# Loads, statistics, transposes and filler matmuls rearranged at the start of an attention and MLP kernel

**Chip, cores, metric.** One NeuronCore of a Trainium2 chip. The metric is the device time of one execution in us; medians are over the runs named. The profile is that of one execution.

## The reference, cut to what matters

One block with adaptive layer norms: grouped-query attention (32 q heads, 8 cached K/V heads, head size 128, 2048 tokens, width 512) and a gated MLP with a spatial matmul.

```python
mod = (silu(c) @ w_mod).reshape(c.shape[0], 6, 1, -1)      # w_mod: 512 x 3072
sa, ca, ga, sb, cb, gb = (mod[:, i] for i in range(6))
h = layernorm(x) * (1 + ca) + sa
x = x + ga * attention(h, k_cache, v_cache, wq, wo)        # q = h @ wq, scores, softmax, @ v, @ wo
h = layernorm(x) * (1 + cb) + sb
x = x + gb * gmlp(h)
```

Before the first score, all of this has to happen: x tile 0 is loaded and normalised, the columns of `sa` and `ca` (a 512 x 1024 part of `w_mod`) are computed, the tile is transposed and modulated, and multiplied with `wq`.

## The kernel before

128 units (8 K/V heads x 16 token tiles) with 8 slots each. In a slot, TensorE (PE) computes 2 QK matmuls of 128x512, ScalarE (ACT) takes the exponential of the 1024 scores, and PE does the PV matmuls of the unit before. What stands in `at(unit, slot, f)` is put ahead of QK in that slot, what stands in `fill[unit, slot]` behind PV. Below, "exp 4" is the exponential of slot 4 of unit 0, if no other unit is named, and a bank is one of the buffers in PSUM into which PE writes. In the traces the work of an engine stands in the order of the program, so what waits holds up what is behind it: the cast of q, whose input is ready at 10.69 us, starts at 11.48, behind the statistics of tile 1.

```python
nc.scalar.dma_start(out=c_bf[:], in_=c_dram)
nc.scalar.dma_start(out=x_sb[:, 0, :], in_=x_dram[:, 0, :])
for i in range(2):                                   # 512 rows of 1 KB each
    part = slice(i * D, (i + 1) * D)
    nc.sync.dma_start(out=wmod_a[:, :, part], in_=wmod_dram[:, :, part])
# ... sync queue then: half of K, wq, x tiles 1 to 3, other half of K, v, the rest of x, wo

warm(14)                                             # matmuls on zeros, results unused
xns0 = ln1_norm(0, 1, ln1_stats(0, 1))
mod_columns(0, wmod_a, 0)                            # 32 matmuls 128x1
ln1_turn(0, 1, xns0, on_act=(1, 3))                  # 4 transposes, modulated on DVE and ACT
# ... 8 transposes of K, copied out by ACT
warm(2)
first["r1"] = ln1_stats(1, 1)                        # tile 1: bn_stats, bn_aggr on DVE, rstd on GpSimd
for fn in qproj(0, list(range(REP)), 0, P, two_engines=True):
    fn()                                             # 16 matmuls; cast half on DVE, half on ACT
first["x1"] = ln1_norm(1, 1, first["r1"])
first["r2"] = ln1_stats(2, 2)
# ...
def first_turn():
    ln1_turn(1, 1, first["x1"])                      # transposes of tile 1
    first["x2"] = ln1_norm(2, 2, first["r2"])
at(0, 1, first_turn)
at(0, 4, lambda: ln1_turn(2, 2, first["x2"]))        # transposes of tiles 2 and 3
fill[0, 0] = [lambda: warm(1)]
fill[0, 2] = [lambda: warm(1)]
fill[0, 3] = qproj(0, list(range(REP)), P, P)        # q of tile 1
fill[0, 6], fill[0, 7], fill[1, 0] = rest_q[0:4], rest_q[4:10], rest_q[10:16]
# ...
ln1_at(1, (1, 1), (1, 5), (1, 7))                    # tiles 4 to 7: statistics, norm, transposes
```

## Time and profile before

| | before |
|---|---|
| median | 1328.3 us (6 runs, 1328.22 to 1329.56) |
| span of the profiled run | 1326.9 us |
| PE busy | 1303.0 us (98%) |
| first QK matmul | 12.33 us |
| first QK of unit 1 | 21.23 us |

From unit 1 on PE has almost no gap, so only the first 30 us matter. A row of the order of time has the start, the duration, the engine (PEld is PE's weight load), the line, the operation, output<-input, the shapes and the count; in brackets the engine's idle time ahead of it and what ended it. The chain and the rows that carry the argument stand in the prediction. One more row, from the order of time of PE in the kernel before, marks the first QK of unit 1:

```profile
21.23 0.59 PE L928 MATMUL s_ps<-qT,kT 128*128 128x512 bf16 x2
```

### The profile page before, as it was taken

The page shows a single profiled execution, that of the slowest core. Times are in us where ns is not written, and L with a number is a line of the kernel's source. Part 1 is how long each engine was busy: PE and PEld are TensorE (multiplying, and loading weights), DVE is VectorE, ACT ScalarE, POOL GpSimd, SP SyncE. Part 2 cuts the span into 40 slices and gives each one's busy share as a digit, 9 for nine tenths or more (in the row PEclk, how much of TensorE's full clock was granted, in tenths as well). Part 3 has the DMA queues.
Part 4 walks back from the last instruction along what each step waited for, and adds up shares of the span by engine and source line. Part 5 has one row for each costly group of instructions (what it writes and reads, how often), then busy time and mean ns, then how long its engine had stood idle before and what let it go on. Part 6 is the DMA issues. An engine that isn't in the chain of part 4 may idle for free.

```text
span 1326.9 us, 27682 instructions
## 1 busy us (share of the span) xinstructions
PE 1303.0 (98%) x12140; PEld 859.3 (65%) x12346; DVE 472.7 (36%) x1166; ACT 1077.4 (81%) x1061; POOL 48.8 (4%) x92
## 2 busy tenths in 40 slices
PE   8999999999999999999999999999999999999997
PEld 5666666666666666666666666666666666644444
DVE  5532222222222222222222222222222566793444
ACT  5898999999999999999999999999999999650000
POOL 1100000000000000000000000000000000120000
PEclk9999999999999999999999999999999999999999
DMA  5461021102111121111110211121101111154200
GB/s 159 102 146 29 17 49 37 33 17 53 21 30 36 34 37 37 29 37 37 33 33 17 53 37 29 21 52 21 33 14 21 25 34 33 29 115 83 64 21 27
DMA packets 146512, 57.59 MB, mean 43 GB/s; under 512 B 136176, under 2 KB 142448, under 8 KB 146384
## 3 DMA queue, kind: packets, MB, share of 16 engines
q1 hardware_dynamic: 139584, 37.19, 14.8%
q0 software_dynamic: 4208, 16.39, 4.5%
q8 instruction: 98, 1.61, 0.5%
q10 hardware_dynamic: 2592, 2.16, 0.5%
q14 instruction: 30, 0.25, 0.1%
HBM read 21.37 MB, written 2.10 MB: 18 GB/s over the span
## 4 chain that ended last, share of the span: by engine, by line
PE 97%; issue 1%; DVE 1%; DMA 1%; ACT 0%; SPq 0%; POOL 0%
PE s_ps L928 35%; PE o_ps L950 35%; PE misc L1290 7%; PE misc L889 7%; PE misc L982 6%; PE s_ps L1136 2%; PE s_ps L1175 2%; PE o_ps L1311 1%; DMA x_sb<-in_A_x_dram 1%; PE s_ps L1311 0%; DVE bnst L691 0%; ACT pT L935 0%; PE misc L1052 0%; DVE qT L901 0%; DVE xn L680 0%
## 5 line engine op out<-in xcount | busy, mean ns | idle before, releaser
L935 ACT ACTIVATE pT<-s_ps 128x1024 bf16<-128x1024 f32 x1024 | 1043.6, 1024 | 86.0 <-PE s_ps L928 11.3
L950 PEld LDWEIGHTS <-pT 128*128 128x128 bf16 x8192 | 548.5, 98 | 241.2
L950 PE MATMUL o_ps<-v,pT 128*128 128x129 bf16 x8192 | 631.5, 220 | 0.0
L928 PE MATMUL s_ps<-qT,kT 128*128 128x512 bf16 x2048 | 608.9, 379 | 12.4 <-ACT qT L903 1.6
L961 DVE RECIPROCAL rall<-o_ps 128x2 f32<-128x2 f32 x256 | 43.6, 170 | 743.9 <-PE o_ps L950 743.8
L928 PEld LDWEIGHTS <-kT 128*128 128x128 bf16 x2048 | 199.3, 98 | 121.8 <-issue 3.6
L889 PE MATMUL misc<-hT,wq_g 128*128 128x512 bf16 (+2 forms) x482 | 167.4, 365 | 0.2
L982 PE MATMUL misc<-wo_g,oT 128*128 128x512 bf16 x385 | 145.9, 379 | 0.0
L962 DVE TENSOR_TENSOR onorm<-o_ps,rall 128x256 bf16<-128x256 f32 x256 | 108.6, 424 | 9.0 <-DVE rall L961 0.3
L1290 PE MATMUL misc<-wsp,z 128*128 128x512 bf16 (+2 forms) x555 | 100.5, 336 | 0.6 <-issue 0.3
L901 DVE CAST qT<-misc 128x512 bf16<-128x512 f32 (+1 forms) x128 | 86.7, 677 | 7.4 <-PE misc L889 7.3
L1290 PEld LDWEIGHTS <-z 128*128 128x128 bf16 x560 | 50.6, 98 | 48.5
L995 DVE TENSOR_TENSOR xacc<-misc,xacc 128x512 f32<-128x512 f32 x112 | 76.0, 679 | 0.0
L889 PEld LDWEIGHTS <-wq_g 128*128 128x128 bf16 x544 | 51.5, 98 | 1.5 <-DMA wq_g<-in_A_wq_dram 0.6
L982 PEld LDWEIGHTS <-oT 128*128 128x128 bf16 x512 | 50.1, 98 | 0.7
L1305 DVE TENSOR_TENSOR gb<-misc,bsp_bc 128x512 bf16<-128x512 f32 (+1 forms) x28 | 18.4, 658 | 59.2 <-PE misc L1290 59.2
L1136 PE MATMUL s_ps<-win_sb,hT 128*128 128x448 bf16 x128 | 27.0, 352 | 0.1
L1146 ACT ACTIVATE z<-s_ps 128x896 bf16<-128x896 f32 x16 | 14.7, 917 | 14.9 <-PE s_ps L1136 14.9
L1175 PE MATMUL s_ps<-hT,win_sb 128*128 128x512 bf16 x109 | 24.3, 379 | 0.2
L691 DVE BATCH_NORM_STATS2 bnst<-x_sb 128x6 f32<-128x512 bf16 x32 | 21.8, 682 | 3.1 <-DMA x_sb<-in_A_x_dram 2.6
L1183 ACT ACTIVATE z1T<-s_ps 128x1024 bf16<-128x1024 f32 x14 | 14.3, 1024 | 10.1 <-PE s_ps L1175 9.1
L708 POOL DMA_DIRECT2D wq_g<-in_A_wq_dram x7 | 5.3, 750 | 420.9 <-PE misc L889 420.9
(79 smaller groups left out, 280.1 us busy)
## 6 DMA issues: line engine op xcount, KB each, us to landing
wq_g<-in_A_wq_dram POOLq DMA_DIRECT2D x7, 512.0 KB, 4.0
v<-in_A_v_cache_dram POOLq DMA_DIRECT2D x7, 512.0 KB, 6.5
wo_g<-in_A_wo_dram POOLq DMA_DIRECT2D x7, 512.0 KB, 4.8
oT<-onorm SPq DMA_TRANSPOSE x128, 2.4
wsp<-in_w_mod_dram POOLq DMA_DIRECT2D x1, 2048.0 KB, 9.3
out_dram<-yout ACTq DMA_DIRECT2D x15, 128.0 KB, 1.7
win_sb<-in_B_w_in_dram POOLq DMA_DIRECT2D x1, 1792.0 KB, 7.7
x_sb<-in_A_x_dram SPq DMA_DIRECT2D x3, 512.0 KB, 6.1
```

Of the source, the lines that this page charges most:

```text
L889: nc.tensor.matmul(ps[0][:, o0 : o0 + n], lhsT=wqs[g][:, dt, hh * DH : (hh + 1) * DH], rhs=hTs[ch][:, dt, c0 : c0 + n], start=(dt == 0), s ...
L901: nc.vector.tensor_copy(out=dst[:, 0:cut], in_=src[:, 0:cut])
L928: nc.tensor.matmul(s_ps[:, h * 512 : (h + 1) * 512].rearrange("p (r q) -> p r q", r=REP), lhsT=groups[g]["kT"][:, kt * P : (kt + 1) * P], ...
L935: nc.scalar.activation(out=pTs[u][:, 2 * i : 2 * i + 2, :], in_=s_ps[:].rearrange("p (k q) -> p k q", k=2), func=ACT.Exp, scale=inv_sqrt_dh,)
L950: nc.tensor.matmul(o_ps[:, hh % 2, 0 : DH + 1], lhsT=pTs[u][:, kt, hh * P : (hh + 1) * P], rhs=groups[g]["v1"][:, kt, 0 : DH + 1], start=( ...
L961: nc.vector.reciprocal(out=rall[:, c0 : c0 + 2], in_=o_ps[:, :, DH])
L962: nc.vector.tensor_tensor(out=onorms[u][:, hh - 1 : hh + 1, :], in0=o_ps[:, :, 0:DH], in1=rall[:, c0 : c0 + 2].unsqueeze(2).to_broadcast([ ...
L982: nc.tensor.matmul(X_ps[:], lhsT=oTs[u][:, hh, :], rhs=groups[g]["wo"][:, hh, :], start=(hh == 0), stop=(hh == REP - 1),)
L995: nc.vector.tensor_tensor(out=xaccs[j][:], in0=X_ps[:], in1=xaccs[j][:], op=ALU.add)
L1136: nc.tensor.matmul(ps[0][:, hf * 512 : hf * 512 + FC], lhsT=h2Ts[j // CT][:, dt, (j % CT) * P : (j % CT + 1) * P], rhs=win_sb[:, dt, FH + ...
L1175: nc.tensor.matmul(ps[0][:, k * 512 : (k + 1) * 512], lhsT=win_sb[:, dt, f * P : (f + 1) * P], rhs=h2Ts[2 * ch2 + k][:, dt, :], start=(dt ...
L1290: nc.tensor.matmul(g_ps[:, :n], lhsT=z2[:, st, f * P : (f + 1) * P], rhs=wsp[t][:, st, c0 : c0 + n], start=(st == 0), stop=(st == NT - 1 a ...
```

## The change

Intent: get x tile 0 and the modulation weight sooner, keep PE's clock up with fillers, and let work that waits stand behind work that is ready.

```diff
-    nc.scalar.dma_start(out=x_sb[:, 0, :], in_=x_dram[:, 0, :])
-    for i in range(2):
-        part = slice(i * D, (i + 1) * D)
-        nc.sync.dma_start(out=wmod_a[:, :, part], in_=wmod_dram[:, :, part])
+    nc.sync.dma_start(out=x_sb[:, 0, :], in_=x_dram[:, 0, :])
+    nc.sync.dma_start(out=wmod_a[:], in_=wmod_dram[:, :, 0 : 2 * D])
...
-    warm(2)
-    first = {}
-    first["r1"] = ln1_stats(1, 1)
+    warm(1)
...
     for fn in qproj(0, list(range(REP)), 0, P, two_engines=True):
         fn()
+    warm(2)
+    first = dict(r1=ln1_stats(1, 1))
+    ln_stats(mv1, 2, x_sb[:, 2, :])
     first["x1"] = ln1_norm(1, 1, first["r1"])
-    first["r2"] = ln1_stats(2, 2)
+    ln_stats(mv1, 3, x_sb[:, 3, :])
+    first["r2"] = rstd_of(mv1[:, 2:4, :], 2, "ln1")
...
-    at(0, 1, first_turn)
-    at(0, 4, lambda: ln1_turn(2, 2, first["x2"]))
-    fill[0, 0] = [lambda: warm(1)]
-    fill[0, 2] = [lambda: warm(1)]
+    at(0, 2, first_turn)
+    at(0, 5, lambda: ln1_turn(2, 2, first["x2"]))
+    for i in (0, 1, 2, 4):
+        fill[0, i] = [lambda: warm(1)]
...
-    fill[0, 6], fill[0, 7], fill[1, 0] = rest_q[0:4], rest_q[4:10], rest_q[10:16]
+    fill[0, 6], fill[0, 7], fill[1, 0] = rest_q[0:5], rest_q[5:11], rest_q[11:16]
```

## The prediction

> **What bounds the kernel now.** I read the page of the whole run first, then the busy time per stretch, and last the order of instructions and the chain that ended last, both in the first 30 us.
>
> ```profile
> span 1326.9 us, 27682 instructions
> PE 1303.0 (98%) x12140; PEld 859.3 (65%) x12346; DVE 472.7 (36%) x1166; ACT 1077.4 (81%) x1061; POOL 48.8 (4%) x92
> ```
>
> TensorE (PE) is busy for 1303.0 of 1326.9 us. The loop is not touched by the change, so at stake are the 23.9 us in which PE is idle. The busy time per stretch says where they lie (first columns: length, then PE):
>
> ```profile
> 0.00:10.00 10.00, 8.44 (x66) 4.11 (x68) 3.40 (x14) 2.74 (x5) 1.69 (x10) 1.00 0.87 249
> 10.00:20.00 10.00, 6.96 (x61) 4.01 (x59) 6.83 (x19) 6.48 (x9) 1.75 (x4) 1.00 1.05 275
> 20.00:30.00 10.00, 9.17 (x94) 6.50 (x92) 6.30 (x16) 8.50 (x10) 1.28 (x2) 1.00 0.01 3
> ```
>
> PE's idle time before 30 us is 1.56 + 3.04 + 0.83 = 5.4 us. In the first stretch most of its busy time is filler, so the useful ceiling is somewhat larger than the idle time there, but all that the change can win is a few us of 1328: 2% would be 26.6 us. The order of time shows what PE waits for (start, duration, engine, line; in brackets the idle time ahead and what ended it):
>
> ```profile
> 9.62 1.07 PE L889 MATMUL misc<-hT,wq_g 128*128 128x128 bf16 x16
> 10.65 0.69 DVE L691 BATCH_NORM_STATS2 bnst<-x_sb 128x6 f32<-128x512 bf16 x1 [1.66 <-DMA x_sb<-in_A_x_dram]
> 11.38 0.18 DVE L692 BATCH_NORM_AGGREGATE mv<-bnst 128x2 f32<-128x6 f32 x1
> 11.48 0.39 DVE L901 CAST qT<-misc 128x256 bf16<-128x256 f32 x1
> 11.90 0.37 ACT L903 CAST qT<-misc 128x256 bf16<-128x256 f32 x1 [1.45 <-DVE qT L901]
> 12.33 0.59 PE L928 MATMUL s_ps<-qT,kT 128*128 128x512 bf16 x2 [1.64 <-ACT qT L903]
> ...
> 17.31 0.38 PE L835 MATMUL misc<-ident,xn 128*128 128x128 bf16 x4 [0.42 <-DVE qT L901]
> ...
> 17.53 1.03 PE L928 MATMUL s_ps<-qT,kT 128*128 128x512 bf16 x4
> 18.16 4.73 ACT L935 ACTIVATE pT<-s_ps 128x1024 bf16<-128x1024 f32 x5 [1.39 <-PE s_ps L928]
> ```
>
> Two stalls. **First:** the q projection ends at 9.62 + 1.07 = 10.69, but VectorE (DVE) casts q only at 11.48, because the statistics of x tile 1 stand ahead of it in DVE's order, and that tile lands only at 10.63. The ScalarE (ACT) half follows the DVE half one after the other, and the first QK matmul starts at 12.33. **Second:** in slot 4 of the first unit the transposes of x tiles 2 and 3 stand ahead of the QK matmul; they wait for the q cast to free a PSUM bank, so ACT has no scores for 1.39 us. That the tile's load lies on the path that ends last, the chain confirms (start, duration):
>
> ```profile
> 3.27 7.36 DMA x_sb<-in_A_x_dram
> 10.65 0.70 DVE bnst L691
> 11.56 0.32 DVE qT L901
> 11.90 0.38 ACT qT L903
> 12.33 0.61 PE s_ps L928 x2
> ```
>
> **What the Trainium skill says.** (1) "TensorE: Matmul & The Clock Gate", Engine queue depths: ScalarE and VectorE are strict FIFO. The trace agrees: DVE's cast, ready at 10.69, waits behind statistics until 11.48. (2) The same page, Part 1: cold matmuls of N=512 start 426.7 ns apart, and the clock rises after one busy window of about 3.4 us, that is free-running. The trace agrees: warm-up matmuls start 0.43 us apart, and full clock is granted from 6.85 us on; it holds through PE's 1.64 us idle. So the fillers are insurance, and here there is no clock loss for them to win back. (3) "DMA: Bandwidth & Descriptors", Issuing engines are not separate DMA queues: another issuing engine saves only sequencer time. So moving x tile 0 to the other queue changes order and not rate. (4) "Perfetto Trace Analysis", DMA Optimizations: DMAs under 2 KB have sizeable overhead. In this trace the rate is 340 to 367 KB/us where rows are 1 KB, and 381 KB/us in the one us (6 to 7) in which the 2 KB rows of K are mixed in, so I expect some 5 to 10% for the modulation weight.
>
> **Part 1, the loads.** x tile 0 (128 KB) goes to the head of the sync queue, ahead of the 1 MB modulation weight, which becomes one load of 512 rows of 2 KB. The bytes ahead of wq are the same. x tile 0 lands at 4.83 today and its normalised form is ready at 7.19; its first reader on PE is at 7.86, after the modulation columns, so it has 0.67 us of slack and its earlier landing (I estimate 3.6, from the first data at 2.1) wins nothing. What PE waits for is the weight. Today its halves land at 5.33 and 7.40, the 32 column matmuls start at 6.99, when the 14 cold warm-ups (14 x 0.427 = 5.98 us) are through, and pause only 0.07 us for the second half. In one piece, nothing may start before all of it is there: behind x tile 0, minus 5 to 10% of about 3 us of transfer, I estimate 7.0 to 7.3. 32 matmuls then take 0.85 us, so they end between 0.1 us earlier and 0.3 us later than now (8.00). I book +0.1 us. wq lands at 9.58 and the last part of h is ready at 9.56; both gate the q projection, so neither alone is worth anything. One sync issue fewer of about 0.65 us, one more of 0.45: the later loads go out 0.2 us sooner, and nobody waits for them.
>
> **Part 2, the statistics go behind the cast.** The cast starts at about 10.73 in place of 11.48: 0.75 us earlier; ACT's half, the first QK (11.58) and the first exp (12.21 for 12.96) move with it. Two fillers of 0.22 us each after the projection lie in PE's wait.
>
> **Part 3, the slots.** The statistics of tile 1 now start after the DVE cast, at 11.04. Today from their start to the normalised tile it is 12.99 - 10.65 = 2.34 us, so this is at 13.38, 0.39 later than today. That is why the transposes move from slot 1 to slot 2. Slots 0 and 1 need only the two score buffers; exp 0 is over at 13.23 and frees the buffer of slot 2, whose QK stands behind transposes (13.42 to 13.65) and starts at 13.65. ACT idles 0.2 us and exp 2 starts at 14.28 (today 14.83). Since only tile 3's statistics are left ahead of h, not those of 2 and 3, h is ready at 15.16 (today 15.59). The second projection follows: its last 13 matmuls and the end take 0.94 us today, so it ends at 16.10 and its cast at 16.82 (today 17.25). QK of slot 4 now stands ahead of the transposes: it starts at about 15.9 and exp 4 at 16.55, for 18.16 today. This is the 1.39 us stall, less a gap of 0.3. The transposes wait until 16.86 for their bank and push QK of slot 5 to 17.1; exp 5 starts at 17.72 (today 19.08), exp 6 at about 18.64, exp 7 at 19.56. The first QK of unit 1, behind exp 6, starts at about 19.9, for 21.23 today: 1.3 us earlier. The remaining q matmuls are only split otherwise (5, 6, 5 for 4, 6, 6).
>
> **Part 4, fillers.** 21 for 18 warm-ups: 3 x 0.22 = 0.65 us more PE work, all in slots where PE waits for exps (0.93 us apart, against 0.43 us of QK). I book 0.
>
> **What carries to the end.** From unit 1 on PE is full, and the next idle time there, near 28.8 us, hangs on DVE work that starts after the last q cast (22.98), so it moves as a whole. No later load is waited for in this stretch. Sum: 1.3 - 0.1 = 1.2 us; 1328.29 - 1.2 = **1327.1 us**, 0.09% faster.
>
> **Rivals.** *A, the weight in one piece lands late:* if row size brings nothing, it lands at 7.4 or after, the whole chain moves by 0.4 us or more and some 0.8 us stay: 1327.5. For: its halves let 16 matmuls begin today. Against: only 0.07 us of wait today. *B, the gain is given back in unit 0 or 1:* slot 2 now waits for the normalised tile, and if DVE is later than I think (statistics, then GpSimd, two handovers), exps 2 and 3 lose what the cast won; or ACT, with 8 exps of 0.93 us, is the bound of unit 1 as well. Then 0.4 us stays: 1327.9. For: ACT is busy 8.50 of 10 us from 20 to 30. Against: PE has 9.17 there. *C, the clock:* if the window falls otherwise, the start runs cold for up to 3.4 us more and a run is 1 us or so longer, in both kernels alike; the three times of before spread by 1.3 us, perhaps for this. With more fillers the changed kernel would suffer less: 1326.5. *D, more is won,* since h or wq come earlier thanks to the larger rows: at most 0.5 us more, 1326.6.
>
> **Range and chances.** The rivals span 1326.5 to 1327.9; the spread of the times of before and of another chip add about 1 us on each side: 1325.8 to 1328.7. All PE idle time before 30 us is 5.4 us, a fifth of the 26.6 us that 2% needs; for a slowdown of that size, nothing is in sight. Faster 0.005, same 0.99, slower 0.005.
>
> **What would show it.** Right: the DVE cast of q at about 10.7 with no DMA wait ahead; the first QK at 11.4 to 11.8; the 1.39 us idle ahead of exp 4 down to 0.3; the first QK of unit 1 at 19.7 to 20.2; the rest of the trace moved as a block. Step 1 is wrong if the column matmuls start after 7.3. Part 3 is wrong if ACT idles over 0.4 us ahead of exp 2. The whole is wrong if the first QK of unit 1 moves by 1.3 us and the span doesn't, or if the clock drops again before 30 us.

## The result

The changed kernel took 1327.24 us (median of 6 runs, 1327.06 to 1328.48) beside 1328.3 us (6 runs) of the kernel before: 1.06 us less. The ratio is 0.9992 (95% interval 0.9979 to 1.0005), "same" by the 2% measure. The ratio goes by mean times (1327.42 over 1328.53), so it is not quite that of the medians. The interval includes 1, and each kernel has one longer run among its six; of the single times, all but one of the changed kernel (1327.06 to 1327.29) lie below the lowest of before (1328.22). A repeat on another chip (below) gave 1326.97 against 1328.6, with all 5 runs below all 9.

Busy time per stretch of the changed kernel (length, then PE, PEld, DVE, ACT, POOL, PE's clock, DMA share, GB/s):

```profile
0.00:10.00 10.00, 7.10 (x63) 3.56 (x65) 3.30 (x14) 2.44 (x5) 1.69 (x10) 1.00 0.84 245
10.00:20.00 10.00, 9.03 (x73) 5.40 (x74) 7.03 (x20) 8.15 (x10) 1.76 (x4) 1.00 1.06 279
20.00:30.00 10.00, 9.16 (x101) 6.64 (x100) 7.23 (x19) 7.44 (x9) 1.28 (x2) 1.00 0.01 4
```

From 10 to 20 us PE went from 6.96 to 9.03 us and ACT from 6.48 to 8.15. In the first 10 us PE has less: the warm-ups ran faster here, since the full clock was granted at 4.59 us and not at 6.85, and PE then waited. (The clock column has 1.00 for the time before the first grant too; there the spacing of the warm-ups, 0.43 us, shows the half speed.) The order of time of the changed kernel:

```profile
7.34 0.95 PE L782 MATMUL misc<-sc_bf,wmod_a 128*128 128x1 bf16 x32 [1.30 <-DMA wmod_a<-in_w_mod_dram]
...
10.83 0.42 DVE L897 CAST qT<-misc 128x256 bf16<-128x256 f32 x1 [1.54 <-PE misc L885]
...
11.17 0.68 DVE L691 BATCH_NORM_STATS2 bnst<-x_sb 128x6 f32<-128x512 bf16 x1
11.29 0.37 ACT L899 CAST qT<-misc 128x256 bf16<-128x256 f32 x1 [0.53 <-DVE qT L897]
11.71 0.59 PE L928 MATMUL s_ps<-qT,kT 128*128 128x512 bf16 x2 [0.49 <-ACT qT L899]
...
13.56 0.40 PE L833 MATMUL misc<-ident,xn 128*128 128x128 bf16 x4 [0.39 <-DVE xn L680]
...
16.72 4.98 ACT L935 ACTIVATE pT<-s_ps 128x1024 bf16<-128x1024 f32 x5 [0.35 <-PE s_ps L928]
...
20.04 0.59 PE L928 MATMUL s_ps<-qT,kT 128*128 128x512 bf16 x2
```

The cast of q is now ended by PE, not by a load's statistics, and the first QK is at 11.71 in place of 12.33 (0.62 us). The transposes of tile 1 hold PE for 0.39 us in slot 2, so by exp 2 (14.43 for 14.83) the lead has shrunk to 0.40 us. The stall ahead of exp 4 is 0.35 us in place of 1.39: exp 4 leads by 1.44 us. The first QK of unit 1 leads by 1.19 us, and the exponentials from the second of unit 1 on by 1.30 us: 1011 of the 1015 exponentials from there on, to 0.01 us. Near the end, the last addition on DVE shows the same distance, before:

```profile
1320.75 0.43 DVE L1327 TENSOR_TENSOR yout<-tmp,x_sb 128x256 bf16<-128x256 f32 x1
```

and after:

```profile
1319.45 0.43 DVE L1327 TENSOR_TENSOR yout<-tmp,x_sb 128x256 bf16<-128x256 f32 x1
```

So nothing after unit 1 answers to the change: it shifts 1.3 ms of work by 1.3 us. The spans of the two profiled runs differ by 1.4 us (1326.9 and 1325.4) and the medians by 1.06; the profiled run of before (1328.74 us) was 0.4 us longer than its usual 1328.3.

### The profile page after: what moved, and what is told of

It is laid out like the page before. It is cut to its first block, busy times and chain, and to the rows that moved or that the text cites. A ratio compares the mean times of both kernels' runs of the same rounds, so it can differ in the third digit from the quotient of the medians.

```text
span 1325.4 us, 27685 instructions
## 1 busy us (share of the span) xinstructions
PE 1302.4 (98%) x12142; PEld 859.2 (65%) x12349; DVE 473.3 (36%) x1166; ACT 1078.4 (81%) x1061; POOL 49.0 (4%) x92
## 3 DMA queue, kind: packets, MB, share of 16 engines
q8 instruction: 98, 1.61, 0.5%
## 4 chain that ended last, share of the span: by engine, by line
PE 97%; issue 1%; DVE 1%; DMA 0%; POOL 0%; ACT 0%; SPq 0%; DVEq 0%
PE s_ps L928 35%; PE o_ps L950 35%; PE misc L885 7%; PE misc L1290 7%; PE misc L982 6%; PE s_ps L1136 2%; PE s_ps L1175 2%; PE o_ps L1311 1%; DMA wmod_a<-in_w_mod_dram 0%; PE s_ps L1311 0%; DVE bnst L691 0%; PE misc L833 0%; DVE xn L680 0%; PE misc L782 0%; PE misc L1052 0%
## 5 line engine op out<-in xcount | busy, mean ns | idle before, releaser
L1183 ACT ACTIVATE z1T<-s_ps 128x1024 bf16<-128x1024 f32 x14 | 14.3, 1024 | 10.1 <-PE s_ps L1175 9.1
```

## The experiments

Twelve kernels in three calls; each call ran on one chip, with 9 runs of the kernel before. The last column counts the runs with a mean granted clock of 0.997 (1 is PE's full speed); why this matters is told under the second experiment. The differences are between medians of 5 and 9 runs; apart from longer ones, the runs of one kernel spread by 0.1 to 0.8 us.

| kernel | median us (5 runs) | before, same chip | difference | 0.997 |
|---|---|---|---|---|
| loads alone | 1328.38 | 1328.44 | -0.06 | 1 of 5 |
| statistics alone | 1329.56 | 1328.44 | +1.12 | 3 of 5 |
| second transposes alone | 1327.66 | 1328.44 | -0.78 | 1 of 5 |
| all slot moves | 1327.33 | 1328.44 | -1.11 | 0 of 5 |
| slots and statistics | 1327.12 | 1328.57 | -1.45 | 0 of 5 |
| changed, weight in halves | 1327.62 | 1328.57 | -0.95 | 1 of 5 |
| changed, no fillers | 1326.87 | 1328.57 | -1.70 | 0 of 5 |
| changed, later transposes in unit 1 | 1326.12 | 1328.57 | -2.45 | 0 of 5 |
| changed, again | 1326.97 | 1328.60 | -1.63 | 0 of 5 |
| changed, tile 0 on its own queue | 1326.84 | 1328.60 | -1.76 | 1 of 5 |
| changed, no fillers, no warm-ups | 1327.84 | 1328.60 | -0.76 | 0 of 5 |
| bundle of four | 1325.36 | 1328.60 | -3.24 | 0 of 5 |

All gave right results. My theory at the start was the prediction's: the order on DVE and PE wins, loads and fillers don't. The rival was that the loads or the first QK carry it.

### Loads alone

The first hunk of the diff, on the kernel before.

> The kernel before with the changed loads alone (x tile 0 at the head of the sync queue, the modulation weight in one load). Theory (all of the gain comes from the order of work on DVE and PE, none from the loads): the q projection ends at 10.8 as after, but the DVE cast still stands behind the statistics of tile 1, whose load lands at about 10.6, so the cast starts at 11.4 to 11.5 and the time stays within 0.15 us of before (1328.3). Rival (the larger rows bring data sooner and this carries through): 0.3 us or more faster.

1328.38 us beside 1328.44: no difference beyond the spread of the runs. The order of time of this kernel shows why (lines are shifted by the edit):

```profile
10.42 0.69 DVE L691 BATCH_NORM_STATS2 bnst<-x_sb 128x6 f32<-128x512 bf16 x1 [1.32 <-DMA x_sb<-in_A_x_dram]
...
11.24 0.39 DVE L899 CAST qT<-misc 128x256 bf16<-128x256 f32 x1
```

The projection was over at 10.60, and the cast still stood behind the statistics of tile 1, which waited for their load. As long as this wait is there, a faster load of the weight can't show. The cast came at 11.24, before the 11.4 to 11.5 expected: tile 1 itself landed at 10.39 for 10.63, and the first QK is at 12.09 for 12.33, exp 0 of unit 4 at 50.36 for 50.58. The medians, 0.06 us apart, don't show these 0.2 us as a gain.

### Statistics alone

```diff
     warm(2)
-    first = {}
-    first["r1"] = ln1_stats(1, 1)
...
-    first["x1"] = ln1_norm(1, 1, first["r1"])
-    first["r2"] = ln1_stats(2, 2)
+    first = dict(r1=ln1_stats(1, 1))
+    ln_stats(mv1, 2, x_sb[:, 2, :])
+    first["x1"] = ln1_norm(1, 1, first["r1"])
+    ln_stats(mv1, 3, x_sb[:, 3, :])
+    first["r2"] = rstd_of(mv1[:, 2:4, :], 2, "ln1")
```

> The kernel before with the statistics of tile 1 moved behind the q cast alone; the transposes stay in slots 1 and 4. Theory (the two moves need each other): the cast starts at 10.75 and the first QK at 11.6, 0.7 us earlier, but the normalised tile 1 comes 0.4 us later (13.4) and now holds back QK of slot 1; exp 1 at about 14.3 in place of 13.91, exp 4 at about 18.4 in place of 18.16, the time some 0.3 us slower than before (1328.6). Rival (the first QK is what the whole hangs on): the 0.7 us stay and the time is 1327.6.

Slower: 1329.56 us in the median, and 1328.85 and 1329.01 in the two runs without a clock of 0.997, that is 0.4 to 0.6 us over before. The order of time:

```profile
11.41 0.59 PE L929 MATMUL s_ps<-qT,kT 128*128 128x512 bf16 x2 [0.92 <-ACT qT L901]
...
13.25 0.52 PE L835 MATMUL misc<-ident,xn 128*128 128x128 bf16 x4 [1.04 <-DVE xn L680]
13.56 1.91 PE L929 MATMUL s_ps<-qT,kT 128*128 128x512 bf16 x4
...
14.66 1.94 ACT L936 ACTIVATE pT<-s_ps 128x1024 bf16<-128x1024 f32 x2 [1.60 <-PE s_ps L929]
```

The first QK is at 11.41, earlier than in the changed kernel, and yet the kernel loses: the transposes of tile 1, still ahead of QK in slot 1, now wait 1.04 us for DVE. The 0.9 us won ahead of exp 0 is gone at exp 1 (14.66, before 13.91). Part of this is a fall of the clock at 13.38 us, told next: from the start of its QK (13.56) to exp 1 it is 1.10 us, in place of 0.63 at full clock. Without these 0.47 us exp 1 would stand at about 14.2 (an estimate), near the 14.3 expected. The mechanism was as expected; the loss was expected at 0.3 us and is 0.4 to 0.6 in the two runs named, which have no sign of such a fall.

This profile shows another thing. These are stretches of 3.41 us of this run; the number after POOL is PE's clock:

```profile
9.97:13.38 3.41, 1.45 (x16) 0.76 (x14) 2.56 (x7) 1.68 (x3) 0.81 (x2) 1.00 1.22 228
13.38:16.80 3.42, 3.42 (x14) 1.46 (x13) 2.32 (x8) 1.94 (x3) 0.95 (x2) 0.50 1.08 342
```

For one stretch of 3.41 us PE ran at half speed, after a stretch in which it was busy for only 1.45 us. How busy PE was does not settle it: in the profile of the next experiment the clock fell after a stretch with 2.38 us,

```profile
5.14:8.55 3.41, 2.38 (x43) 1.50 (x42) 1.17 (x6) 0.00 (x0) 0.81 (x2) 1.00 1.05 361
8.55:11.96 3.41, 3.19 (x27) 2.86 (x27) 1.42 (x4) 1.77 (x3) 0.23 (x1) 0.50 1.29 236
```

and in the kernel before it did not fall after one with 1.77 us (10.26 to 13.67). The mean clock of this run is 0.997; the runs with 0.997 are 0.5 to 1.4 us above the median of the other runs of their kernel. So a run with 0.997 is a run in which the clock fell once, as far as the two profiles that caught it show. The reverse isn't shown: the mean also counts a stretch at half speed after PE's last matmul, 5.9 us long in the profile of before (from 1320.98 us) and 2.5 us in that of the bundle below. With a short stretch there, a fall at the start would still leave 0.998, so the counts of 0.997 may be too low. Some longer runs had 0.998 (one of the kernel with later transposes, at 1327.41; one of the halves, at 1328.99; one without warm-ups, at 1328.8); whether these hide a fall stays open.

### Second transposes alone

```diff
-    at(0, 4, lambda: ln1_turn(2, 2, first["x2"]))
+    at(0, 5, lambda: ln1_turn(2, 2, first["x2"]))
```

> The kernel before with one edit: the transposes of x tiles 2 and 3 move from slot 4 to slot 5 of unit 0. Theory (the 1.39 us stall ahead of exp 4 is most of what was won): first QK at 12.33 as before, exp 4 at about 17.0 in place of 18.16, exp 5 at about 18.15, first QK of unit 1 at about 20.2 to 20.3 and the time 0.9 to 1.0 us faster than before (1327.3), nearly all of the gain. Rival (the statistics behind the cast win most, the slots the rest): 0.5 us faster or less.

1327.66 us in the median; the four runs with a clock above 0.997 took 1326.99 to 1327.75, their median 1327.48, against 1328.44: 0.96 us. One line gives most of the gain. The order of time:

```profile
16.97 0.59 PE L928 MATMUL s_ps<-qT,kT 128*128 128x512 bf16 x2
...
17.40 0.90 PE L835 MATMUL misc<-ident,xn 128*128 128x128 bf16 x8
17.60 1.02 ACT L935 ACTIVATE pT<-s_ps 128x1024 bf16<-128x1024 f32 x1 [0.17 <-PE s_ps L928]
```

QK of slot 4 goes ahead, the transposes wait behind it for their bank, and ACT idles 0.17 us in place of 1.39. In this very profile the clock had fallen from 8.55 to 11.96 us, so that the first QK came at 13.03, 0.7 us later than before; the first QK of unit 1 was at 20.92, still earlier than the 21.23 of before.

### All slot moves

Both `at` lines and the split 5, 6, 5, on the kernel before, with the statistics still ahead of the cast.

> The kernel before with all slot moves (transposes in slots 2 and 5, remaining q matmuls split 5, 6, 5), statistics still ahead of the cast. Theory: the move of the first transposes from slot 1 to 2 wins nothing by itself, since tile 1 is ready at 12.99 either way; the split 5, 6, 5 takes one 0.11 us matmul out of unit 1, where PE is full. So 0.1 us better than with the second transposes moved alone: 1.0 to 1.1 us faster than before (1327.2). Rival: the same as before or 0.5 us faster, if the gain hangs on the earlier first QK.

1327.33 us, 1.11 us less than before: as expected, and 0.15 us better than the four undisturbed runs of the one-line kernel, which is less than the spread of either. The traces show the split's part: from exp 0 to exp 1 of unit 1 it is 1.43 us here, and 1.54 in the one-line kernel and before. With the first QK at 12.29, as late as before, exp 4 starts at 16.96 and the first QK of unit 1 at 20.28. The rival, that all hangs on the first QK, is refuted by this and by the run with the statistics alone.

### Slots and statistics, loads and fillers of before

> The kernel before with the statistics behind the cast and with all slot moves, but with the loads and fillers of before. Theory (loads and fillers win nothing in runs without a clock drop; together with the slots the statistics win 0.1 to 0.3 us more): 1327.0 to 1327.2, not slower than the changed kernel, in runs without a drop; the drop (granted clock 0.997) may come more often than with the changed kernel's fillers. Rival (the loads are part of the gain): 1327.5 or more without a drop.

1327.12 us beside 1328.57: 1.45 us less, 0.34 us more than with the slots alone (across two chips, each against its own before). In the traces exp 0 of unit 4 stands at 49.31 for 49.52 with the slots alone. So together with the slot moves the statistics behind the cast win some 0.2 to 0.3 us, where alone they lost. What the new loads add to this is taken up in the part on the prediction.

### The changed kernel without fillers

```diff
-    warm(1)
...
-    warm(2)
...
-    for i in (0, 1, 2, 4):
-        fill[0, i] = [lambda: warm(1)]
```

> The changed kernel without any filler after the 14 warm-ups (7 of 21 warm-ups gone). In earlier runs a profile with the clock at half speed for one stretch of 3.41 us between 8 and 17 us had a granted clock of 0.997 and was about 1 us longer; others had 0.998 or 0.999. Theory (fillers keep that drop away, and cost nothing themselves): runs without the drop are as the changed kernel (1327.2), but at least 3 of 5 runs show the drop and take 1328.2 to 1328.6. Rival A (the fillers do nothing): at most 1 of 5 shows it, median 1327.2. Rival B (the fillers stand in the way): runs without the drop are 0.3 us faster, 1326.9.

1326.87 us, and none of 5 runs had a clock of 0.997. The theory that fillers keep the clock drop away fell in this form: at least 3 of 5 runs were expected to show it. Of 11 runs of the changed kernel one had it; of 27 runs of before, three. Five runs are too few to tell such shares apart, so whether the fillers lower the chance stays open. That they cost nothing is shown: from the first QK to the first QK of unit 1 it is 8.32 us here (11.44 to 19.76), and 8.33 us with all of them (11.71 to 20.04). The rival "in the way" seems to fit the time, 0.3 us less than expected, but not these distances: what is earlier here is the weight, which landed at 7.03 us and not at 7.30. The changed kernel with all its fillers, run again (below), took 1326.97.

### The changed kernel with the weight in two halves

> The changed kernel with the modulation weight loaded in two halves by columns again (x tile 0 still at the head of the sync queue). Theory (in one piece the load holds back all 32 column matmuls until 7.30): the first 16 run ahead, the columns end at about 7.9 in place of 8.29, the q projection starts on wq at about 9.5 and ends at 10.6 to 10.7 in place of 10.79; 0.1 to 0.2 us faster, 1327.1. Rival (2 KB rows land enough sooner to pay for it): 0.1 us or more slower, as the second half lands at 7.5 or later.

1327.62 us, 0.75 us more than the kernel without fillers on the same chip; without its two longer runs (1328.52 with a clock of 0.997, and 1328.99) it took 1327.49 to 1327.62, still 0.6 us more. My theory fell and the rival holds. The halves landed at 6.23 and 7.60 us, wq at 9.94 (without fillers: 7.03 and 9.33), and the first QK was at 11.97 for 11.44. Rows of 1 KB and one more issue on the sync queue (0.62 to 0.69 us each) together cost more than the early half wins; which of the two costs more was not separated. So behind tile 0 on the sync queue, one load of 2 KB rows is worth keeping, once the cast no longer waits for tile 1.

### The changed kernel again, and with tile 0 on its own queue

The first is the changed kernel itself; the second has one edit:

```diff
-    nc.sync.dma_start(out=x_sb[:, 0, :], in_=x_dram[:, 0, :])
+    nc.scalar.dma_start(out=x_sb[:, 0, :], in_=x_dram[:, 0, :])
```

> The changed kernel itself once more, as a control beside the next three on one chip. In every profile so far with the weight in one load and the statistics behind the cast, the first QK starts 4.41 us after the weight lands (7.30, 7.16, 7.03 to 11.71, 11.57, 11.44) and the first QK of unit 1 8.32 to 8.33 us after that. Theory: the same two distances here, and a time between 1326.9 and 1327.3 by where the load lands; runs with a clock drop at 1328.2 to 1328.6. Rival: other distances, so that something else decides.

> The changed kernel with x tile 0 back on the ACT queue and the weight, still in one load of 2 KB rows, at the head of the sync queue. Theory (it is the row size that helps the changed kernel and the place behind x tile 0 that costs it: in its trace the DMA moved 158, then 100 KB/us between 2 and 4 us, the weight's data only starting): the weight lands 0.2 to 0.4 us sooner, first QK 4.41 us after it, the time 0.2 to 0.4 us below the control. Rival (bytes decide, not order): lands within 0.1 us of the control, same time.

The control: weight landed at 7.18, first QK at 11.60 (4.42 us later), first QK of unit 1 at 19.93 (8.33 us later), 1326.97 us. So in these profiles all that follows moves with the landing of the weight (wq lands 2.2 us after it each time). With tile 0 on the ACT queue it landed at 6.89, 0.29 us sooner, though the bytes are the same; first QK at 11.33 (4.44 us later), 8.33 us to unit 1, and the exponentials of unit 4 lead the control by 0.27 us. The time, 1326.84 us, is 0.13 us less, where 0.2 to 0.4 was expected; the runs' own spread of 0.4 us leaves its size uncertain. DMA in single us tells where the 0.29 us come from. The changed kernel, as first profiled (the last column is GB/s):

```profile
2.00:3.00 1.00, 1.00 (x4) 0.44 (x3) 0.17 (x1) 0.44 (x1) 0.00 (x0) 1.00 0.95 163
3.00:4.00 1.00, 1.00 (x4) 0.32 (x3) 0.63 (x5) 0.21 (x1) 0.00 (x0) 1.00 0.72 102
...
5.00:6.00 1.00, 1.00 (x5) 0.29 (x3) 0.12 (x1) 0.00 (x0) 0.76 (x2) 1.00 1.05 377
```

With tile 0 on the ACT queue:

```profile
2.00:3.00 1.00, 1.00 (x4) 0.44 (x3) 0.17 (x1) 0.99 (x2) 0.00 (x0) 1.00 0.71 125
3.00:4.00 1.00, 1.00 (x4) 0.32 (x3) 0.68 (x4) 0.12 (x1) 0.00 (x0) 1.00 0.80 273
...
5.00:6.00 1.00, 1.00 (x4) 0.45 (x3) 0.44 (x1) 0.00 (x0) 0.00 (x0) 1.00 1.06 413
```

Behind tile 0 on one queue the weight starts late, and between 3 and 4 us only 102 GB/s move; on two queues it is 273. The issue of the weight shows it too, in the changed kernel

```profile
1.19 0.69 SPq L698 DMA_DIRECT2D wmod_a<-in_w_mod_dram  x1
```

and with tile 0 on the ACT queue:

```profile
0.73 0.69 SPq L698 DMA_DIRECT2D wmod_a<-in_w_mod_dram  x1
```

It comes 0.46 us sooner, since the sync engine has no other issue ahead of it. That alone can account for the 0.29 us; whether the order within the queue costs anything more was not tested. From 5 to 6 us rows of 2 KB move at 377 to 413 GB/s, where the kernel before, with 1 KB rows, has 353. The theory holds for the landing: the place behind x tile 0 costs 0.29 us of it. The row size was not varied alone.

### The transposes of tiles 4 to 7 one slot later

```diff
-    ln1_at(1, (1, 1), (1, 5), (1, 7))
+    ln1_at(1, (1, 1), (1, 5), (2, 0))
```

> The changed kernel with the same kind of move once more: the transposes of x tiles 4 to 7, which stand ahead of QK in slot 7 of unit 1 and wait for DVE (PE idles 0.56 us and three times about 0.1 to 0.2 us from 27.0 to 28.5, and ACT idles 2.16 us), move to slot 0 of unit 2. Theory (a transposition that waits ahead of QK stalls PE, and PE is the bound from there on): PE has 0.9 us of QK and PV work in that wait, so about 0.8 us faster than the changed kernel, 1326.4. Rival (the wait only moves on, since the next q projection needs these transposes at once): the same as the changed kernel, 1327.2.

1326.12 us, 0.75 us less than the kernel without fillers on the same chip. The order of time of PE in the changed kernel,

```profile
26.36 0.61 PE L950 MATMUL o_ps<-v,pT 128*128 128x129 bf16 x8
27.53 1.87 PE L833 MATMUL misc<-ident,xn 128*128 128x128 bf16 x16 [0.56 <-DVE xn L680]
```

and with the later transposes:

```profile
26.70 0.59 PE L928 MATMUL s_ps<-qT,kT 128*128 128x512 bf16 x2
27.12 0.61 PE L950 MATMUL o_ps<-v,pT 128*128 128x129 bf16 x8
27.58 1.67 PE L833 MATMUL misc<-ident,xn 128*128 128x128 bf16 x16
```

A whole QK and PV round now stands in what was PE's wait, and the transposes start without one. From the first QK of unit 1 to exp 0 of unit 4 it is 28.36 us in place of 29.24: 0.88 us. It is the same move as the one in slot 4 of unit 0, and pays about the same.

### A bundle of four edits

Tile 0 on the ACT queue, no fillers after the 14 warm-ups, the later transposes, and:

```diff
-                cut = len(hs) // 2 if two_engines else len(hs)
-                nc.vector.tensor_copy(out=dst[:, 0:cut], in_=src[:, 0:cut])
                 if two_engines:
-                    nc.scalar.copy(out=dst[:, cut:], in_=src[:, cut:])
+                    nc.scalar.copy(out=dst, in_=src)
+                else:
+                    nc.vector.tensor_copy(out=dst, in_=src)
```

> Four edits together on the changed kernel: loads as in the run before this one, no fillers after the 14 warm-ups, the transposes of x tiles 4 to 7 in slot 0 of unit 2, and the first q cast whole on ACT, so that DVE takes the statistics of tile 1 as soon as it lands. Theory: the later transposes win 0.9 us as measured, the ACT cast ends 0.2 us sooner than the two halves one after the other and lets tile 1 be ready some 0.5 us sooner (0.4 us at exp 4), the loads 0.2 us; fillers 0. Sum 1.5 us below the control, about 1325.6. Rival (after the first QK another wait takes over): only the 0.9 us of the later transposes stay, 1326.2.

1325.36 us (5 runs, 1325.35 to 1325.44): 1.61 us less than the changed kernel on the same chip and 3.24 us less than before; the ratio to before is 0.9975 (0.9961 to 0.9989), the only interval here, besides that of the later transposes (0.997 to 0.9997), that leaves out 1. It beats both kernels, by 0.1 us more than the sum expected. The order of time:

```profile
10.12 0.69 DVE L691 BATCH_NORM_STATS2 bnst<-x_sb 128x6 f32<-128x512 bf16 x1 [1.12 <-DMA x_sb<-in_A_x_dram]
10.54 0.58 ACT L896 CAST qT<-misc 128x512 bf16<-128x512 f32 x1
...
11.18 1.02 PE L926 MATMUL s_ps<-qT,kT 128*128 128x512 bf16 x4 [0.67 <-ACT qT L896]
...
15.75 4.98 ACT L933 ACTIVATE pT<-s_ps 128x1024 bf16<-128x1024 f32 x5 [0.17 <-PE s_ps L926]
```

The cast in one piece on ACT takes 0.58 us, where the two halves took 0.83 (10.83 to 11.66), as ACT's half waited for DVE's. The statistics of tile 1 no longer wait for the cast, nor the cast for them. Exp 4 leads the control by 0.85 us, and exp 0 of unit 4 by 1.74 us. The traces split the 1.74: the weight lands 0.36 us sooner (6.82 for 7.18), from there to the first QK it is 0.06 less, from the first QK to that of unit 1 0.43 less (7.90 for 8.33), and from there to unit 4 0.89 less (28.35 for 29.24). The last part goes with the later transposes, as in their own run; the 0.43 with the cast on ACT, if the fillers cost nothing as above. No run has this cast alone.

### Without warm-ups

The kernel without fillers, and without its 14 warm-ups.

> The changed kernel without fillers and without the 14 warm-ups as well. Theory (the 14 warm-ups are what lifts the clock in time, the later fillers add little): TensorE runs at half speed until the middle of unit 0 or so, the q projection of 0.9 us takes about 1.8 us, the first QK starts 1.0 us or more later and the time is 1.0 to 3.0 us above the control. Rival (the clock does not matter, since the start waits for DMA, DVE and ACT): within 0.3 us of the control.

1327.84 us, 0.87 us more than the control. The weight landed at 7.13, the clock was granted only at 10.98 us, and the first projection took from 9.56 to 11.30 (1.74 us; control 9.47 to 10.68, 1.21 us). The first QK was at 12.22, 5.09 us after the weight in place of 4.42. So the warm-ups ahead of the weight are worth 0.7 to 0.9 us: the theory in kind, but below the 1.0 to 3.0 us expected. PE was at full speed before the first QK, not in the middle of unit 0.

## Why the prediction was right

It forecast 1327.1 us and 1327.24 was measured; its mechanism holds, and its sum nearly. That the two agree to 0.14 us is in part luck: the gain was 1.06 us here and 1.63 on another chip for a forecast of 1.2, and within the profiles a late start of 0.13 us and the 0.11 us of the split, booked as 0, nearly cancel. By its steps:

1. **What is at stake** (the idle time of PE in the first 30 us, all else shifts as a block): right. The shift is 1.30 us from the second exponential of unit 1 to the end.
2. **Part 1, loads, booked at +0.1 us.** In the first pair of profiles it was so: landing 7.30 (estimate 7.0 to 7.3), columns over at 8.29 for 8.00, projection over at 10.79 for 10.69. By its own sign ("if the column matmuls start after 7.3") this step failed by a hair: they started at 7.34. Whether the new loads cost or win stays open. One pair on one chip speaks for a win: the kernel with the new loads (no fillers) had its first QK at 11.44 and 1326.87 us, the one with the old loads 11.74 and 1327.12, but their runs overlap. Over the profiles with warm-ups and no fall of the clock up to there, four with the loads of before and five with those of the change, one load lands earlier than the second half (mean 7.15 for 7.35), but with all 32 matmuls still to do the columns end 0.99 to 1.00 us after it in place of 0.59 to 0.62, and the projection ends at 10.65 for 10.66 in the mean. At the head of its queue (two profiles, of them one the bundle) one load has it over at 10.41 and 10.51. That tile 0's own landing (3.05) wins nothing was right.
3. **Part 2, the cast**: 10.83 for the predicted 10.73, first QK 11.71 for 11.58.
4. **Part 3, the slots**: exp 2 at 14.43 (14.28), exp 4 at 16.72 (16.55), exp 5 at 17.88 (17.72), exp 7 at 19.71 (19.56), first QK of unit 1 at 20.04 (19.9). All of them are late by the 0.13 us of the first QK, give or take 0.04; each further step that can be read off was right. What the working did not say, and the experiments did: of some 1.1 to 1.6 us, the one-line move of the second transposes gives 0.96 alone, and moving the statistics alone loses 0.4 to 0.6.
5. **Split 5, 6, 5**: called "only split otherwise", booked 0. The lead grows from 1.19 to 1.30 us just where unit 1 has one 0.11 us matmul less, in a stretch in which PE has no gap, and the kernel with the slot moves alone shows the same 0.11.
6. **Part 4, fillers, booked 0**: right for their cost (8.32 and 8.33 us). That the clock "holds" was read from one run. It falls in some runs, and costs 0.5 to 1.4 us then; whether the added fillers make this rarer is open.
7. **Rivals**: A (a late weight) was seen to be the thing that decides the single run, 4.4 us before the first QK; B did not come; C is real, but for 3.4 us within the first 17 us and not at the start alone; D's number came near on another chip (1326.97), but its reason isn't shown, as the projection ended no sooner in the mean.

## What to carry to other kernels

When PE is the bound and its queue is in order, look at every instruction that waits for another engine, and ask what ready work stands behind it: moving transposes behind one QK matmul won 0.96 us in one place and 0.75 us in the other, at the cost of one line each. Starting the first stage sooner won nothing by itself, as the next wait in order ate it; it paid, by some 0.2 to 0.3 us, only once the transposes were moved, while the slot moves paid alone (1.11 us). An effect of 0.1% can be read from block shifts in two traces, if the start of a stretch (here the weight's landing) is subtracted first, since it moves by up to 0.27 us (7.03 to 7.30) between profiles with the same loads.

## What the Trainium skill lacked or had wrong

- "TensorE: Matmul & The Clock Gate", Part 1 and the last table of the page: the clock is said to fall after an idle window of about 3.4 us, and the advice is no PE gap over about 3 us. Keeping to that was not enough here: the clock fell to 0.50 for one window of 3.41 us after windows with PE busy for 1.45 and for 2.38 of 3.41 us, whose longest gap was 1.04 us. In the kernel before a window with 1.77 us busy, and in the one without warm-ups one with 1.66, did not bring it down. How busy a window has to be the page doesn't say, and these runs don't settle it either.
- "DMA: Bandwidth & Descriptors", Issuing engines are not separate DMA queues: issuing from several engines "will only save the time on the sequencer". The runs don't contradict it, and give a size for the cold start, which the page lacks: with a 128 KB load on the other queue and not ahead of it, the 1 MB load was issued 0.46 us sooner (0.73 for 1.19) and landed 0.29 us sooner with equal bytes.
